# A planner that counts DMA landings later, keeps row loads and expert weights apart, and starts with the first q and k

## The chip, the cores and the metric

The kernel runs on one core of one Trainium2 chip. The metric is the device time of the program in microseconds (us). Three runs of the kernel before gave 535.44, 537.68 and 540.07 us; the median, 537.68, is what the change is measured against.

## The reference

Two stages, one behind the other. The first is attention over 8 batches, 8 heads, 576 positions and 64 channels, masked by blocks of 64; the second is a noisy top-2 router over 8 experts with two layers each.

```python
scores = q @ k.T / sqrt(64), masked where block(i) < block(j); attn = softmax(scores)
x = (attn @ v) as 4608 rows of 512
noisy = x @ w_gate + log1p(exp(x @ w_noise)) * noise
top2 = the two largest of noisy per row, with softmax weights over the two
out[row] = sum over its two experts e of weight * (relu(x[row] @ w1[e]) @ w2[e])
```

w1[e] is 512x1024, w2[e] is 1024x512, all inputs and the output are float32; the kernel computes its products in bfloat16.

## The kernel before

**Attention** goes through the batches 0 to 7. For each batch, six loads of q and k (`load_qk`, chunks c = 0, 1, 2) go out on GpSimd's queue (POOL) with a cast to bfloat16 into eight "raw" buffers; TensorE (PE) turns them (`turn`), VectorE (DVE) or ScalarE (ACT) copies the turned chunk to SBUF as Tq and Tk (`turn_copy`). V comes in five pieces on SyncE's queue (SP) as float32 into three "vst" buffers (`load_v`), and DVE or POOL casts each piece (`cast_v`). PE makes scores in twelve units and one small rest unit per batch, ACT takes their exponentials (`exps`), DVE zeroes the masked blocks (`mask`, L424), PE multiplies with V (`av_mm`, L439 and L449), DVE divides (`av_out`).

**Router.** After each pair of batches DVE computes the top two and every row's place in the list of its expert; POOL scatters each row twice into a table in DRAM (`scatter`, L586), xd[0] for batches 0 to 3 (half 0) and xd[1] for batches 4 to 7 (half 1). Behind each row lies a record of 16 bytes. The ends of the lists are cleared beforehand by eight DMAs from SP for each half (`clear_x`).

**Experts.** Each of 16 steps handles one expert for one half, in the order (0,0), (0,1), (0,2), (1,0), (1,1), (1,2), then (0,e), (1,e) for e = 3 to 7. A step loads 640 rows transposed from xd (`load_x`, L612, SP, two "xg" buffers), runs eight layer-1 groups of eight matmuls (`layer1`, L659) with a relu each (L668), and five layer-2 tiles (`layer2`, L675). The first product of a token is scaled (`y_early`, L683, ACT or DVE, three "y" buffers) and stored to DRAM by SP (`y_store`, L690); the second gathers the first by POOL (`gather`, L699), adds it on DVE (`y_late`, L710) and is scattered to the output by POOL (`y_out`, L717). The records of a half are read once (`load_rec`, L617, SP) and turned into row numbers and weights by DVE (`read_rec_a`, L625 to L634, and `read_rec_b`). Expert weights come in four loads each on POOL's queue with a cast to bfloat16 (`load_w`, L333); experts 0 to 2 have buffers of their own during attention, later ones reuse the space of attention.

**The order of the work** is not written by hand. `Plan` is a list scheduler that runs while the program is built: each operation has an engine (or a choice of two), a cost, operations that it comes after, buffers that it takes and gives, and a key (lower goes first). A DMA holds its engine for its cost, then its transfer takes `xfer` on one of two "wires" (POOL's or the rest), starting 1.2 after the issue, and counts as landed 1.0 after the wire is done. `behind` waits for another operation's start, `calm` holds an operation back while its wire is booked further ahead than that number. The planned times give only the order of each engine's instructions. On the chip an instruction waits for data and for buffers, never for a planned time; each engine takes its instructions strictly in that order, so one that waits holds up all behind it.

Of the kernel before, what the change touches and what calls it, by code (L numbers as in the profile page):

```python
# [19 lines left out]
class Plan:  # L20
# [4 lines left out]


    HOP = 0.08
    ISSUED = 1.2
    LANDED = 1.0
    WIDE = 1.15  # L30

# [3 lines left out]

    def add(self, eng, cost, fn=None, after=(), key=0.0, take=(), give=(), xfer=None, behind=(), calm=None):
        eng = () if eng is None else (eng,) if isinstance(eng, str) else tuple(eng)
        self.ops.append(dict(eng=eng, cost=cost, fn=fn, key=key, take=tuple(take), give=tuple(give),
                             xfer=xfer and xfer / self.WIDE, calm=calm, left=0, outs=[], next=[], start=None, by=None))
        n = len(self.ops) - 1  # L40
        for field, named in (("outs", after), ("next", behind)):
            for a in set(x for x in named if x is not None):
                self.ops[a][field].append(n)
                self.ops[n]["left"] += 1
        return n

    def order(self):
        ops, free = self.ops, dict(self.pools)
        busy, ready, marks, ends = {}, {}, [], []
        wire = {True: 0.0, False: 0.0}  # L50

        def put(n):
# [6 lines left out]
        def may(o):  # L59
            if o["calm"] is not None and wire[o["eng"][0] == "POOL"] - t > o["calm"]:  # L60
                return False
            return all(free[p] > 0 for p in o["take"])

        def begin(n, t, e):
# [13 lines left out]
            if o["xfer"] is not None:  # L78
# [6 lines left out]
                end = wire[q] + self.LANDED  # L85
            heapq.heappush(ends, (end if e is None else end + self.HOP, n))

# [3 lines left out]
        t = 0.0  # L91
        while True:
# [37 lines left out]
            if ends:  # L130
                t = ends[0][0]
            elif any(ready.values()) and t < max(wire.values()):
                t = max(wire.values())
            else:
                break
# [7 lines left out]
def kernel(  # L143
# [100 lines left out]
    zeros = [zrow[32 * i:32 * i + 32, 0:4 * DR] for i in range(4)]  # L244

    def setup_first():
        make_identity(nc, ident)
# [348 lines left out]

    def clear_x(half):
        flat = xd[half].rearrange("(e r) c -> e r c", e=E)[:, ZR:CAP, :].rearrange("e (p a) c -> e p (a c)", a=4)
        for e in range(E):
            nc.sync.dma_start(out=flat[e], in_=zeros[e % 4])  # L600

# [161 lines left out]

    UB = 3 * HP + 1

    def unit(b, n):
# [3 lines left out]

    add("POOL", 0.6, setup_first, key=-100)
    o_pool = add("POOL", 2.0, setup_pool, key=-30)
    o_vec = add("DVE", 2.5, setup_vector, key=-1)
# [11 lines left out]
    xr_new = {}  # L785
    prev_router = None
    av_all, noi = {}, {}
    qk_free = {}
    last_units = []
# [4 lines left out]
    for b in range(B):  # L794
# [7 lines left out]
        for c in range(3):  # L802
            for x in "qk":
                ld = add("POOL", 0.76 if c < 2 else 0.6, lambda b=b, x=x, c=c: load_qk(b, x, c),
                         key=u0 - 20 + c, take=["raw"], xfer=1.6 if c < 2 else 0.4,
                         after=[units[b - 2, (2, 0)]] if b > 1 else [])
                turned[x, c] = ld
        need = {0: u0, 1: u0 + 3, 2: u0 + 6}
        got = {}
        for c in range(2):  # L810
            for x in "qk":
                pe = add("PE", 0.55, lambda b=b, x=x, c=c: turn(b, x, c), after=[turned[x, c], o_new],
                         key=need[c] - 5, take=["tr"], give=["raw"])
                n = got[x, c] = add(("DVE", "ACT"), (1.04, 1.0), None, after=[pe], key=need[c] - 5, give=["tr"])
                pl.ops[n]["fn"] = lambda b=b, x=x, c=c, n=n: turn_copy(b, x, c, pl.ops[n]["by"])
        pe = add("PE", 0.6, lambda b=b: turn_rest(b), after=[turned["q", 2], turned["k", 2], o_new],
                 key=need[2] - 5, take=["tr"], give=["raw", "raw"])
# [4 lines left out]
        for idx in range(5):  # L822
            ld = add("SP", 0.15, lambda b=b, idx=idx: load_v(b, idx), key=u0 - 20 + idx, take=["vst"],
                     xfer=1.2 if idx < 4 else 0.6, after=[units[b - 2, (0, 0)]] if b > 1 else [])
            n = cast[idx] = add(("POOL", "DVE"), (0.62, 0.5) if idx < 4 else (0.7, 0.6), None,
                                after=[ld, o_vb], key=u0 - 2, give=["vst"])
            pl.ops[n]["fn"] = lambda b=b, idx=idx, n=n: cast_v(b, idx, pl.ops[n]["by"])
        o_nz = add("SP", 0.2, lambda b=b: load_nz(b), key=u0, xfer=0.6,
                   after=[units[b - 1, (1, 0)]] if b else [o_cast])
# [3 lines left out]
        for n, un in enumerate(UNITS):  # L833
            key = u0 + n
            if un == "r":
                s = add("PE", 0.4, lambda b=b: scores_rest(b), key=key, take=["sc"], after=list(got.values()))
                units[b, "r"] = add("ACT", 0.44, lambda b=b: exps_rest(b), key=key, after=[s, o_e4], give=["sc"])
                continue
# [7 lines left out]
            if m >= 3:  # L846
                deps += [got["r"]]
            s = add("PE", 0.4, lambda b=b, m=m, p=p: scores(b, m, p), key=key, take=["sc"], after=deps)
            units[b, (m, p)] = add("ACT", 1.05, lambda b=b, m=m, p=p: exps(b, m, p), key=key,
# [28 lines left out]
        add(None, 0, key=u0, after=[pes[0, 4], pes[1, 4]], give=["esc4"])  # L878
        add(None, 0, key=u0, after=[units[b, (3, 2)]], give=["qk"])

        kr = u0 + UB + 1
# [22 lines left out]
        if b % 2:  # L904
# [7 lines left out]
            add(None, 0, key=kr, after=[rw, sh], give=["rt"])  # L912
            ss = [add("POOL", 1.0, lambda pb=pb, t=t, i=i: scatter(pb, t, i), after=[rw, sh], key=kr + (20 if b < 7 else 0),
                      xfer=0.36)
# [3 lines left out]
        if b % BH == BH - 1:  # L918
            tot = add("PE", 0.2, lambda half=half: totals(half), after=[sh], key=kr + 1, take=["av"])
            done_b[half] = add("DVE", 0.2, lambda half=half: totals_copy(half), after=[tot], key=kr + 1, give=["av"])  # L920
    for half in range(NH):
        add("SP", 0.8, lambda half=half: clear_x(half), key=2, after=[units[half, (2, 0)], o_vec], xfer=2.8)

# [25 lines left out]
    o_top = add(None, 0, open_top, key=0, after=end_av)  # L949
    rec_ops = {}  # L950
    for half in range(NH):
        lr = add("SP", 0.2, lambda half=half: load_rec(half), key=unit(6, 6) + 0.5, after=scat_ops[half], xfer=3.0)
        ra = add("DVE", 1.6, lambda half=half: read_rec_a(half), key=unit(6, 0), after=[lr, done_b[half], o_cast])
        rec_ops[half] = add("DVE", 1.8, lambda half=half: read_rec_b(half), key=unit(6, 0), after=[ra])
    st_ops = {i: [] for i in range(NH)}
    l2_of, wmarks = {}, {}
    last_g = last_2 = last_x = last_h = None
    for sn, (half, e) in enumerate(SEQ):
        kb = 1000 + 20 * sn
        lx = add("SP", 0.2, lambda half=half, e=e: load_x(half, e), key=unit(6, 6) + sn, take=["xg"],  # L960
                 after=scat_ops[half], behind=[last_x], xfer=3.7)
        last_x = lx
        o_h = add(None, 0, key=kb, take=["hs"], after=[lx, last_h])
        last_h = o_h
# [211 lines left out]
```

## Time and profile before

| | |
|---|---|
| median of 3 runs | 537.68 us |
| the profiled execution | 536.13 us, span 534.4 us |
| busy over the span | PE 419.3, POOL 287.0, ACT 256.2, PE weight loads 260.5, DVE 180.5 us |
| mean granted TensorE clock | 0.886 |
| DMA | 96.22 MB landed, mean 180 GB/s; 104384 of 143642 packets under 512 B |

The profile is of one execution. Its page cuts the span into 40 slices of 13.4 us, each digit the busy share of an engine in tenths. The other views used are: the timeline (start, length, engine, line, operation, tile, and in brackets how long the engine stood idle before it and what released it); the list of waits (engine, line, what it waited for, us in total, times, longest); and windows (busy time of each engine in a stretch, then the granted clock of TensorE as a share of full speed, the mean busy share of the 16 DMA engines, which passes 1 when packets of two queues overlap, and GB/s). PE is TensorE's matmuls, PEld its weight loads, SPq and POOLq the queues' own DMA issues.

### The profile page before, as it was taken

How to read it: one execution, taken by the hardware profiler on the slowest of the kernel's cores; microseconds unless marked ns; L12 is line 12 of the kernel's file. 1: busy time of each engine (PE TensorE's matmuls, PEld its weight loads, DVE VectorE, ACT ScalarE, POOL GpSimd, SP SyncE). 2: the span in 40 equal slices, each digit the busy share in tenths (PEclk: the TensorE clock that was granted, in tenths of full speed). 3: DMA queues.
4: the chain of work that ended last, by engine and by line, in shares of the span. 5: the costliest groups of instructions: out<-in, count | busy, mean ns of one | idle time of the engine just before them, and what ended most of it. 6: DMA issues, size and time to landing. Idle time of an engine off the chain costs nothing.

```text
span 534.4 us, 10377 instructions
## 1 busy us (share of the span) xinstructions
PE 419.3 (78%) x4092; PEld 260.5 (49%) x4111; DVE 180.5 (34%) x486; ACT 256.2 (48%) x344; POOL 287.0 (54%) x327
## 2 busy tenths in 40 slices
PE   2588777887760199979997979489959979999990
PEld 1366555655530077635654626255435545565550
DVE  3477588578560264013211121002113212112220
ACT  2478777488651066534534525155233534555220
POOL 7134357678724742776633656347544554557560
PEclk9779889589755589999999989879979989999996
DMA  9999997896999999859999697977949986677440
GB/s 163 185 204 164 192 208 170 192 196 174 231 98 135 157 149 159 247 127 203 200 236 210 132 214 110 203 151 211 206 145 209 206 229 203 209 226 233 148 136 32
DMA packets 143642, 96.22 MB, mean 180 GB/s; under 512 B 104384, under 2 KB 121792, under 8 KB 143584
## 3 DMA queue, kind: packets, MB, share of 16 engines
q0 software_dynamic: 38496, 54.74, 50.6%
q1 hardware_dynamic: 105088, 40.73, 37.5%
q8 instruction: 34, 0.56, 0.5%
q14 instruction: 24, 0.20, 0.1%
HBM read 80.56 MB, written 48.41 MB: 241 GB/s over the span
## 4 chain that ended last, share of the span: by engine, by line
PE 45%; DMA 25%; issue 9%; POOL 6%; DVE 5%; ACT 4%; SPq 3%; POOLq 0%; ACTq 0%; DVEq 0%
PE hp L659 19%; PE yp L675 17%; DMA yd<-ysb 7%; DMA rc<-xd 6%; DMA vst<-in_v_dram 5%; POOL xd L586 3%; DMA raw<-in_k_dram 3%; ACT esc L403 2%; PE av L439 2%; DMA raw<-in_q_dram 2%; DMA gbuf<-yd,grow 2%; PE sc L394 2%; POOL out_dram L717 2%; PE av L449 1%; SPq L612 1%
## 5 line engine op out<-in xcount | busy, mean ns | idle before, releaser
L659 PE MATMUL hp<-xg,w 128*128 128x320 bf16 x1024 | 150.8, 308 | 21.2 <-ACT hsb L668 21.2
L675 PE MATMUL yp<-w,hsb 128*128 128x512 bf16 x621 | 144.4, 385 | 10.6 <-DVE yo L710 9.6
L710 DVE SCALAR_TENSOR_TENSOR yo<-yp,wrow,gbuf 128x512 f32<-128x512 f32 x70 | 52.3, 750 | 252.8 <-ACT ysb L683 119.2
L659 PEld LDWEIGHTS <-w 128*128 128x128 bf16 x1024 | 102.3, 100 | 67.7 <-issue 22.2
L668 ACT ACTIVATE hsb<-hp 128x640 bf16<-128x640 f32 x128 | 89.6, 704 | 64.8 <-PE hp L659 64.4
L717 POOL DMA_INDIRECT out_dram<-yo,trow x70 | 70.8, 1011 | 92.2 <-DVE yo L710 73.7
L403 ACT ACTIVATE esc<-sc 128x1024 bf16<-128x1024 f32 x96 | 93.5, 1026 | 28.8 <-PE sc L394 28.5
L675 PEld LDWEIGHTS <-hsb 128*128 128x128 bf16 x640 | 63.1, 99 | 85.8 <-issue 17.7
L683 ACT ACTIVATE ysb<-yp,wrow 128x512 f32<-128x512 f32 x69 | 47.4, 687 | 111.4 <-PE yp L675 72.9
L586 POOL DMA_INDIRECT xd<-xr,slots x72 | 72.1, 1001 | 46.0 <-DVE ms L571 22.1
L699 POOL DMA_INDIRECT gbuf<-yd,grow x70 | 72.9, 1042 | 38.1 <-issue 21.4
L439 PE MATMUL av<-vt,esc 128*128 128x65 bf16 x640 | 31.4, 207 | 28.6 <-DVE esc L424 23.7
L394 PE MATMUL sc<-Tq,Tk 64*128 64x512 bf16 (+4 forms) x320 | 41.1, 343 | 15.2 <-ACT esc L403 7.4
L439 PEld LDWEIGHTS <-esc 128*128 128x128 bf16 x640 | 25.9, 106 | 36.6 <-DVE esc L424 24.8
L344 PE MATMUL tr<-ident,raw 128*64 128x128 bf16 x512 | 26.8, 265 | 19.0 <-DMA raw<-in_q_dram 15.7
L459 DVE TENSOR_TENSOR xr<-av,rden 128x256 bf16<-128x256 f32 (+1 forms) x80 | 33.9, 424 | 4.0 <-DMA xd<-xr,slots 1.2
L333 POOL DMA_DIRECT2D w<-in_moe_w_dram x32 | 25.2, 795 | 15.0 <-DMA w<-in_moe_w_dram 10.0
L344 PEld LDWEIGHTS <-raw 128*64 128x64 bf16 x512 | 20.7, 137 | 25.7 <-DMA raw<-in_q_dram 16.3
L312 POOL CAST vt<-vst 128x512 bf16<-128x512 f32 x14 | 8.5, 616 | 41.2 <-DMA vst<-in_v_dram 15.7
L394 PEld LDWEIGHTS <-Tk 64*128 64x128 bf16 x320 | 13.1, 100 | 27.2 <-issue 13.8
L458 DVE RECIPROCAL rden<-av 128x4 f32<-128x4 f32 (+1 forms) x80 | 14.1, 177 | 14.3 <-PE av L439 9.6
L449 PE MATMUL av<-vt,esc 128*64 128x65 bf16 x320 | 15.4, 211 | 4.0 <-DVE noisy L507 3.6
(120 smaller groups left out, 230.0 us busy)
## 6 DMA issues: line engine op xcount, KB each, us to landing
yd<-ysb SPq DMA_DIRECT2D x70, 256.0 KB, 2.9
w<-in_moe_w_dram POOLq DMA_DIRECT2D x32, 512.0 KB
vst<-in_v_dram SPq DMA_DIRECT2D x32, 256.0 KB, 7.9
raw<-in_q_dram POOLq DMA_DIRECT2D x16, 256.0 KB
raw<-in_k_dram POOLq DMA_DIRECT2D x16, 256.0 KB
xd<-gbuf SPq DMA_DIRECT2D x16, 130.0 KB, 7.2
xd<-xr,slots POOLq DMA_INDIRECT x72
gbuf<-yd,grow POOLq DMA_INDIRECT x70
```

Source lines behind the costliest of these rows:

```text
L344: nc.tensor.transpose(tp[64 * f:64 * f + 64, r * P:(r + 1) * P], raw[:, f, r * D:(r + 1) * D], ident)
L394: nc.tensor.matmul(out=sc[:, f, off:off + z - a], lhsT=kT[sl, m * S + jt * P:m * S + (jt + 1) * P], rhs=qT[sl, m * S + a:m * S + z], start ...
L403: nc.scalar.activation(out=escs[b, st][:, mm, :, piece * 512:(piece + 1) * 512], in_=scs.pop((b, m, piece)), func=AF.Exp, scale=scale)
L439: nc.tensor.matmul(out=av[:, f, mm, :], lhsT=esc[:, mm, f, c:c + P], rhs=vb[:, jt, h, :], start=(jt == 0), stop=(jt == idx))
L586: ins = nc.gpsimd.indirect_dma_start(out=xd[half].bitcast(I32), out_offset=bass.IndirectOffsetOnAxis(ap=slots[:, pb * TG + t, i:i + 1], ax ...
L659: nc.tensor.matmul(out=hp[:, n, 0:NW], lhsT=wload[e, 1][:, db, fb * P:(fb + 1) * P], rhs=xgs[half, e][:, db, n * NW:(n + 1) * NW], start=( ...
L668: nc.scalar.activation(out=o, in_=i, func=AF.Relu)
L675: nc.tensor.matmul(out=yp, lhsT=hs[half, e][:, fb, c * P:(c + 1) * P], rhs=wload[e, 2][:, fb, :], start=(fb == 0), stop=(fb == FB - 1))
L683: nc.scalar.activation(out=t, in_=yps[half, e, c], func=AF.Copy, scale=w)
L699: ins = nc.gpsimd.indirect_dma_start(out=g, out_offset=None, in_=yd[half][0:e * CAP], in_offset=bass.IndirectOffsetOnAxis(ap=grow[half][:, ...
L710: nc.vector.scalar_tensor_tensor(out=t, in0=yps[half, e, c], scalar=wrow[half][:, e, c:c + 1], in1=gslot.pop((half, e, c)), op0=ALU.mult, ...
L717: ins = nc.gpsimd.indirect_dma_start(out=out, out_offset=bass.IndirectOffsetOnAxis(ap=trow[half][:, e, c:c + 1], axis=0), in_=yos.pop((hal ...
```

## The change

The planner gets two more numbers for an operation. `late` is added to the planned landing of a DMA: 2.0 for q, k, V, noise and weight loads, 1.5 for stores and gathers of the first products, 3.0 for row loads, 5.0 for the record load. `kind` marks row loads of the first four steps ("x") and weight loads ("w"): in the plan none of one kind starts before the last of the other has landed, and a weight load also stands back while a row load could start. Weights of experts 1 and 2 are planned behind the row loads of the second and third step; the condition `calm` of expert 0's goes from 2 to 4. Row loads and record loads now cost SP 4.0 in the plan instead of 0.2. POOL starts with the two first loads (q and k, c = 0), then the identity matrix, the other four loads of batch 0, and then the constants; V of batch 0 is planned after the first turns, and q and k of batch 1 behind V of batch 0. The clears become single operations at batch 1 (half 0) and batch 4 (half 1) with `calm`, scatters wait for them and are planned 4.0 after their row numbers, and scores of a batch stand behind the rest unit of the batch before. What is computed, the DMAs and their sizes are the same.

```diff
-    WIDE = 1.15
+    WIDE = 1.1
...
         def may(o):
             if o["calm"] is not None and wire[o["eng"][0] == "POOL"] - t > o["calm"]:
+                return False
+            if o["kind"] and last["w" if o["kind"] == "x" else "x"] > t:
+                return False
+            if o["kind"] == "w" and any(ops[n]["kind"] == "x" and ops[n]["start"] is None and
+                                        all(free[p] > 0 for p in ops[n]["take"]) for _, n in ready.get("SP", ())):
                 return False
...
                 end = wire[q] + self.LANDED
-            heapq.heappush(ends, (end if e is None else end + self.HOP, n))
+                if o["kind"]:
+                    last[o["kind"]] = max(last[o["kind"]], end)
+            heapq.heappush(ends, (end + o["late"] + (0.0 if e is None else self.HOP), n))
...
-    add("POOL", 0.6, setup_first, key=-100)
-    o_pool = add("POOL", 2.0, setup_pool, key=-30)
+    o_ident = add("POOL", 1.2, setup_ident, key=-50)
+    o_first = add("DVE", 2.2, setup_first, key=-50)
+    o_pool = add("POOL", 2.0, setup_pool, key=-17)
...
                 ld = add("POOL", 0.76 if c < 2 else 0.6, lambda b=b, x=x, c=c: load_qk(b, x, c),
-                         key=u0 - 20 + c, take=["raw"], xfer=1.6 if c < 2 else 0.4,
-                         after=[units[b - 2, (2, 0)]] if b > 1 else [])
+                         key=u0 - 20 + c if b or c else -100, take=["raw"], xfer=1.6 if c < 2 else 0.4, late=LATE,
+                         after=[units[b - 2, (2, 0)]] if b > 1 else [], behind=[v_last] if b == 1 else [])
...
-            ld = add("SP", 0.15, lambda b=b, idx=idx: load_v(b, idx), key=u0 - 20 + idx, take=["vst"],
-                     xfer=1.2 if idx < 4 else 0.6, after=[units[b - 2, (0, 0)]] if b > 1 else [])
+            ld = v_last = add("SP", 0.45, lambda b=b, idx=idx: load_v(b, idx), key=u0 - 20 + idx, take=["vst"],
+                              xfer=1.2, late=LATE, after=[units[b - 2, (0, 0)]] if b > 1 else [] if b else [turn0],
+                              behind=[v_last])
...
+        if b % BH == 1 - half:
+            cleared = [add("SP", 0.3, lambda half=half, e=e: clear_x(half, e), key=u0 + 5 + e,
+                           after=[units[b, (2, 0)], o_vec], xfer=0.36, calm=2.0) for e in range(E)]
...
-            ss = [add("POOL", 1.0, lambda pb=pb, t=t, i=i: scatter(pb, t, i), after=[rw, sh], key=kr + (20 if b < 7 else 0),
+            routed = add(None, 4.0, after=[rw, sh])
+            ss = [add("POOL", 1.05, lambda pb=pb, t=t, i=i: scatter(pb, t, i), after=[routed, *cleared], key=kr + (20 if b < 7 else 0),
...
-    for half in range(NH):
-        add("SP", 0.8, lambda half=half: clear_x(half), key=2, after=[units[half, (2, 0)], o_vec], xfer=2.8)
...
-                       behind=[prev, marks[n]], calm=calm, xfer=(2.7, 3.1)[n // 2])
+                       behind=[prev, marks[n]], calm=calm, xfer=3.3, late=2.0, kind="w")
-    for e in range(NWE):
-        weights(e, lambda: wE, [units[2 + e, (m, 0)] for m in range(4)], unit(6, 0) + e)
...
-        lr = add("SP", 0.2, lambda half=half: load_rec(half), key=unit(6, 6) + 0.5, after=scat_ops[half], xfer=3.0)
+        lr = add("SP", 4.0, lambda half=half: load_rec(half), key=unit(6, 6) + 0.5, after=scat_ops[half], xfer=3.0, late=5.0)
...
+    weights(0, lambda: wE, [units[2, (m, 0)] for m in range(4)], unit(6, 0), calm=4)
...
-        lx = add("SP", 0.2, lambda half=half, e=e: load_x(half, e), key=unit(6, 6) + sn, take=["xg"],
-                 after=scat_ops[half], behind=[last_x], xfer=3.7)
+        lx = add("SP", 4.0, lambda half=half, e=e: load_x(half, e), key=unit(6, 6) + sn, take=["xg"],
+                 after=scat_ops[half], behind=[last_x], xfer=3.7, late=3.0, kind="x" if sn < 4 else None)
         last_x = lx
+        if sn in (1, 2):
+            weights(sn, lambda: wE, [lx] * 4, unit(6, 0) + sn)
...
-                            after=st_ops[half] + [rec_ops[half]], behind=[last_g], xfer=0.7)
+                            after=st_ops[half] + [rec_ops[half]], behind=[last_g], xfer=0.7, late=1.5)
...
-                new.append(add("SP", 0.15, lambda half=half, e=e, c=c: y_store(half, e, c), after=[ye],
-                               key=kb, give=["y"], xfer=0.7))
+                new.append(add("SP", 0.35, lambda half=half, e=e, c=c: y_store(half, e, c), after=[ye],
+                               key=kb, give=["y"], xfer=0.7, late=1.5))
```

## Rows read from the trace of the kernel before

**Rows 1.** The page's 40 slices: PE's busy share and the DMA engines', in tenths

```profile
PE   2588777887760199979997979489959979999990
DMA  9999997896999999859999697977949986677440
```

**Rows 2.** The timeline around the long stop of PE, SP's queue first, then POOL, DVE, PE

```profile
146.27 6.21 SPq L612 DMA_TRANSPOSE xg<-xd  x1
152.53 5.79 SPq L617 DMA_DIRECT2D rc<-xd  x1
...
148.29 1.43 POOL L333 DMA_DIRECT2D w<-in_moe_w_dram  x2
...
179.95 0.82 POOL L333 DMA_DIRECT2D w<-in_moe_w_dram  x1
...
183.25 0.22 DVE L625 TENSOR_SCALAR rf<-rc 128x120 f32<-128x120 int32 x1 [24.06 <-DMA rc<-xd]
...
184.88 0.84 PE L439 MATMUL av<-vt,esc 128*128 128x65 bf16 x12 [23.44 <-DVE esc L424]
```

**Rows 3.** Windows of 4 us: busy us of each engine, then clock, DMA share, GB/s

```profile
152.00:156.00 4.00, 1.89 (x26) 1.46 (x26) 3.18 (x14) 0.00 (x0) 0.00 (x0) 0.50 1.34 79
156.00:160.00 4.00, 2.88 (x25) 1.29 (x25) 2.60 (x15) 3.99 (x6) 0.89 (x1) 0.50 1.43 58
184.00:188.00 4.00, 3.12 (x43) 2.13 (x44) 3.42 (x16) 0.38 (x1) 3.39 (x4) 0.50 1.18 213
216.00:220.00 4.00, 4.00 (x21) 1.84 (x20) 0.00 (x0) 1.38 (x2) 3.08 (x4) 1.00 1.05 344
228.00:232.00 4.00, 4.00 (x23) 2.08 (x22) 0.00 (x0) 1.71 (x3) 2.95 (x3) 1.00 0.47 166
```

**Rows 4.** The timeline of the second record load and its reader

```profile
236.04 0.38 SPq L617 DMA_DIRECT2D rc<-xd  x1
...
243.26 0.42 DVE L625 TENSOR_SCALAR rf<-rc 128x120 f32<-128x120 int32 x1
```

**Rows 5.** The line of the row loads: time from issue to landing over all 16

```profile
DMA to landing us min/median/max: 4.8/10.7/25.7
```

**Rows 6.** The page's DMA issues: the weight loads

```profile
w<-in_moe_w_dram POOLq DMA_DIRECT2D x32, 512.0 KB
```

**Rows 7.** The timeline of PE where the second step's first layer begins

```profile
209.00 1.25 PE L659 MATMUL hp<-xg,w 128*128 128x320 bf16 x8
```

**Rows 8.** The timeline of the start: SP, POOL, DVE, and PE's turns and scores

```profile
0.92 2.02 SPq L301 DMA_DIRECT2D vst<-in_v_dram  x3
...
3.33 0.91 POOL L291 DMA_DIRECT2D raw<-in_q_dram  x1
...
5.97 1.12 DVE L312 CAST vt<-vst 128x512 bf16<-128x512 f32 x3
...
8.83 1.06 PE L344 MATMUL tr<-ident,raw 128*64 128x128 bf16 x16 [8.83 <-DMA raw<-in_q_dram]
...
14.82 1.06 PE L344 MATMUL tr<-ident,raw 128*64 128x128 bf16 x16
22.27 1.04 PE L394 MATMUL sc<-Tq,Tk 64*128 64x512 bf16 x6 [6.39 <-DVE Tq L355]
```

**Rows 9.** The list of PE's waits: PE behind the relu's output

```profile
PE hp L659 <- ACT hsb L668: 21.2, 5, 8.7
```

**Rows 10.** The timeline of one such stop: SP's row load, ACT, PE

```profile
328.16 8.78 SPq L612 DMA_TRANSPOSE xg<-xd  x1
...
346.31 0.69 ACT L683 ACTIVATE ysb<-yp,wrow 128x512 f32<-128x512 f32 x1 [11.10 <-DMA yd<-ysb]
...
348.77 1.49 PE L659 MATMUL hp<-xg,w 128*128 128x320 bf16 x5 [8.66 <-ACT hsb L668]
```

**Rows 11.** The list of all waits: VectorE's casts behind V

```profile
DVE vt L312 <- DMA vst<-in_v_dram: 13.8, 4, 10.2
DVE vt L316 <- DMA vst<-in_v_dram: 13.1, 8, 2.6
```

More of the change, by code (lines that the diff above doesn't have):

```diff
@@ L34, in __init__, with add @@
         self.pools = dict(pools)
-    def add(self, eng, cost, fn=None, after=(), key=0.0, take=(), give=(), xfer=None, behind=(), calm=None):
+    def add(self, eng, cost, fn=None, after=(), key=0.0, take=(), give=(), xfer=None, behind=(), calm=None, late=0.0, kind=None):
         eng = () if eng is None else (eng,) if isinstance(eng, str) else tuple(eng)
         self.ops.append(dict(eng=eng, cost=cost, fn=fn, key=key, take=tuple(take), give=tuple(give),
-                             xfer=xfer and xfer / self.WIDE, calm=calm, left=0, outs=[], next=[], start=None, by=None))
+                             xfer=xfer and xfer / self.WIDE, calm=calm, late=late, kind=kind, left=0, outs=[], next=[], start=None, by=None))
         n = len(self.ops) - 1
@@ L50, in order @@
         wire = {True: 0.0, False: 0.0}
+        last = {"x": 0.0, "w": 0.0}
         def put(n):
@@ L131, in order @@
                 t = ends[0][0]
-            elif any(ready.values()) and t < max(wire.values()):
-                t = max(wire.values())
+            elif any(ready.values()) and t < max(*wire.values(), *last.values()):
+                t = max(*wire.values(), *last.values())
             else:
@@ L244, with setup_ident @@
     zeros = [zrow[32 * i:32 * i + 32, 0:4 * DR] for i in range(4)]
+    def setup_ident():
+        make_identity(nc, ident)
     def setup_first():
-        make_identity(nc, ident)
         for i in range(2):
@@ L595, in scatter, with clear_x @@
         scat[half].append(ins.ins.name)
-    def clear_x(half):
+    def clear_x(half, e):
         flat = xd[half].rearrange("(e r) c -> e r c", e=E)[:, ZR:CAP, :].rearrange("e (p a) c -> e p (a c)", a=4)
-        for e in range(E):
-            nc.sync.dma_start(out=flat[e], in_=zeros[e % 4])
+        nc.sync.dma_start(out=flat[e], in_=zeros[e % 4])
     xgs, hs, hps, yps, ysb, yos, grow, trow, wrow = ({} for _ in range(9))
@@ L764 @@
     UB = 3 * HP + 1
+    LATE = 2.0
     def unit(b, n):
@@ L785 @@
     xr_new = {}
-    prev_router = None
+    prev_router = v_last = None
     av_all, noi = {}, {}
-    qk_free = {}
+    rest = {}
     last_units = []
@@ L811 @@
             for x in "qk":
-                pe = add("PE", 0.55, lambda b=b, x=x, c=c: turn(b, x, c), after=[turned[x, c], o_new],
+                pe = add("PE", 0.55, lambda b=b, x=x, c=c: turn(b, x, c), after=[turned[x, c], o_new, o_ident],
                          key=need[c] - 5, take=["tr"], give=["raw"])
+                if c == 0:
+                    turn0 = pe
                 n = got[x, c] = add(("DVE", "ACT"), (1.04, 1.0), None, after=[pe], key=need[c] - 5, give=["tr"])
                 pl.ops[n]["fn"] = lambda b=b, x=x, c=c, n=n: turn_copy(b, x, c, pl.ops[n]["by"])
-        pe = add("PE", 0.6, lambda b=b: turn_rest(b), after=[turned["q", 2], turned["k", 2], o_new],
+        pe = add("PE", 0.6, lambda b=b: turn_rest(b), after=[turned["q", 2], turned["k", 2], o_new, o_ident],
                  key=need[2] - 5, take=["tr"], give=["raw", "raw"])
@@ L822 @@
         for idx in range(5):
-            ld = add("SP", 0.15, lambda b=b, idx=idx: load_v(b, idx), key=u0 - 20 + idx, take=["vst"],
-                     xfer=1.2 if idx < 4 else 0.6, after=[units[b - 2, (0, 0)]] if b > 1 else [])
+            ld = v_last = add("SP", 0.45, lambda b=b, idx=idx: load_v(b, idx), key=u0 - 20 + idx, take=["vst"],
+                              xfer=1.2, late=LATE, after=[units[b - 2, (0, 0)]] if b > 1 else [] if b else [turn0],
+                              behind=[v_last])
             n = cast[idx] = add(("POOL", "DVE"), (0.62, 0.5) if idx < 4 else (0.7, 0.6), None,
-                                after=[ld, o_vb], key=u0 - 2, give=["vst"])
+                                after=[ld, o_vb, o_first], key=u0 - 2, give=["vst"])
             pl.ops[n]["fn"] = lambda b=b, idx=idx, n=n: cast_v(b, idx, pl.ops[n]["by"])
-        o_nz = add("SP", 0.2, lambda b=b: load_nz(b), key=u0, xfer=0.6,
+        o_nz = add("SP", 1.0, lambda b=b: load_nz(b), key=u0, xfer=0.4, late=LATE,
                    after=[units[b - 1, (1, 0)]] if b else [o_cast])
@@ L835 @@
             if un == "r":
-                s = add("PE", 0.4, lambda b=b: scores_rest(b), key=key, take=["sc"], after=list(got.values()))
+                s = rest[b] = add("PE", 0.4, lambda b=b: scores_rest(b), key=key, take=["sc"], after=list(got.values()))
                 units[b, "r"] = add("ACT", 0.44, lambda b=b: exps_rest(b), key=key, after=[s, o_e4], give=["sc"])
@@ L847 @@
                 deps += [got["r"]]
-            s = add("PE", 0.4, lambda b=b, m=m, p=p: scores(b, m, p), key=key, take=["sc"], after=deps)
+            s = add("PE", 0.4, lambda b=b, m=m, p=p: scores(b, m, p), key=key, take=["sc"], after=deps,
+                    behind=[rest.get(b - 1)])
             units[b, (m, p)] = add("ACT", 1.05, lambda b=b, m=m, p=p: exps(b, m, p), key=key,
```

## The prediction

> **What bounds the kernel now.** I read the page's slices first, to find where PE, with 419 us the busiest engine, is not busy. Three places stand out [rows 1]: the first two slices, slice 13 (160 to 174 us, digit 0), and single digits of 4, 5 and 7 in the second half. The DMA digits show something else: nearly 9 throughout until the last quarter, so transfers are a resource to be shared, and a gain in one place may be taken back in another.
>
> The timeline around slice 13 names the stop [rows 2]. PE stands for 23.44 us behind the mask at L424. The mask needs nothing new; it is queued on DVE behind the first instruction of the record reader (L625), which waits 24.06 us for the record load. SP issued the first row load at 146.27 and the record load at 152.53; DVE was at L625 at 183.25 - 24.06 = 159.2, and the records were there at 183.25, 37.0 us after the first row load began. Why so late: POOL issued two weight loads of expert 1 at 148.29, into the middle of the row load. The windows show what the mixture does [rows 3]: from 152 to 160 the engines are fully booked (share 1.34 and 1.43) and land only 79 and 58 GB/s, against 344 GB/s at 216. The comparison is the second record load, with no weight load beside its first microseconds: issued at 236.04, its reader ran at 243.26 without a wait, so it took at most 7.2 us [rows 4].
>
> **The change, part by part.** The sum is against the profiled execution, 536.13 us, which stands 1.55 below the median.
>
> *The record wait.* Two edits act on it. The plan's own numbers (order only, no times of the chip): before, the records count as landed 0.2 + 1.2 + 3.7/1.15 + 3.0/1.15 + 1.0 = 8.2 after the first row load starts; now the row load holds SP for 4.0, the record load ends at 8.0, its wire at 8.0 + 1.2 + 3.0/1.1 = 11.9, landing with 1.0 and `late` 5.0 at 17.9. So L625 moves some 9.7 back in DVE's order, behind mask and divisions that no longer stand behind it. And weights of expert 1 can't be planned before the second row load has landed: 8.0 + 4.0 + 1.2 + 3.7/1.1 + 1.0 = 17.6 after the first began, instead of 2 us after it. Apart, a row load took 4.8 us at best and 10.7 in the median [rows 5], the record load 7.2 at most: records at 12 to 18 us after the first row load. DVE used to arrive at 12.9 and now arrives near 22.6. The wait goes: **-23.4**, lower gains under the rivals.
>
> *The clock behind it.* PE's granted clock was 0.50 (1.2 GHz) through the stop and still in 184 to 188, with 3.12 us of matmuls [rows 3]; at full clock these take half. **-1.5** (0 to -3).
>
> *Weights late.* What is late next is expert 1. Before, its four loads went out from 148.29 to 179.95 [rows 2], and PE began the second step at 209.00 [rows 7], 62.7 after the first row load. Without the stop PE arrives at 62.7 - 23.4 = 39.3. Loads that start at 17.6 at the old spacing, (179.95 - 148.29)/3 = 10.6 each, would end near 17.6 + 31.7 + 3 = 52: 13 us late. Four loads land 4 x 512 KB [rows 6]; at the 166 GB/s of an ordinary stretch [rows 3] that is 12.6: ready near 31, early. The range is 0 to +13; I take **+4**, nearer the unmixed end, because the mixing is what the edit ends.
>
> *The start.* POOL now issues q and k before its constants; q went out at 3.33 and PE turned it at 8.83, 5.5 later [rows 8]. From about 0.9 that gives 6.4: -2.4. SP has no data to wait for, so V's first loads still go out at 0.92 beside q; "ahead of V" holds in the plan alone. The identity's two POOL instructions, behind two issues, are hidden by the wait for q. Six q and k issues now precede the constants; DVE's cast of these comes later, while DVE has nothing else. Then PE stood 6.39 us because DVE held V's casts ahead of the copy to Tq; its turn was over at 15.88 and scores came at 22.27. With V counted 2.0 later, copies come first: up to -6.4. Against it: V's three buffers were emptied from 5.97 on; casts placed behind the copies come some 8 us later, and so do the next V loads. Range -9 to +8; I take **-3**, as the engines are booked from the first slice [rows 1].
>
> *First products in the expert stage.* PE waited 21.2 us in five stops for a relu [rows 9]. In one of them a row load held SP's queue for 8.78 us from 328.16, the stores came behind it, ACT stood 11.10 us for a free store buffer with the next step's relus behind it, and PE stood 8.66 [rows 10]. The plan saw none of that: a row load cost 0.2, a store landed 0.15 + 1.2 + 0.7/1.15 + 1.0 = 3.0 after its turn. Now the row load costs 4.0 and the store lands 1.5 later, so the fourth product is planned behind two or so relus of the next step, each of which feeds 1.09 us of PE work (the plan's cost of a group). Five stops by 2.2 is 11; all 21.2 at most; a worse order could cost 5. I take **-6**, half of the 11, because moved products delay others.
>
> *V's ring.* Casts stand later everywhere. DVE waits 26.9 us in all for V [rows 11]; most of the lateness is time that was waited before. **+2** (0 to +36, see below).
>
> *At nothing:* the clears (same sixteen DMAs, at other batches; V's landings cover them; 0 to +3 if V stands behind them), expert 0's `calm` of 4 (the same four loads, earlier, beside q and k; 0 to +4), `routed` and the wait of scatters for the clears (done long before), scores behind the rest unit (same order). The end of the kernel is untouched.
>
> Sum: -23.4 - 1.5 + 4 - 3 - 6 + 2 = -27.9; 536.13 - 27.9 + 1.55 = **510**.
>
> **The rivals.** *Apart on paper only (R1).* Nothing on the chip makes POOL wait for the row loads. If POOL reaches expert 1's weights while they are in flight, records come 37.0 after the start again, DVE arrives at 22.6, and 14.4 us of waiting remain: -9.0, with the other terms -1 + 0 - 3 - 6 + 2: 537.7 - 17 = **521**. Against it: POOL has the scatters of the third pair ahead, which wait for the router; for it: planned and real times differ everywhere.
>
> *The same bytes (R2).* The record wait is traded one for one for PE waiting on expert weights, and the relus' stops stay: all else but the clock returned, 537.7 - 1.5 = **536**. For it: booked engines [rows 1]. Against it: 58 GB/s in the mixture against 344 apart, and a share of 0.47 at 228 [rows 3], room that later work can use. The Trainium skill (DMA: Bandwidth & Descriptors, "Issuing engines are not separate DMA queues") speaks for R2: DMAs from different issuing engines run on the same 16 DMA engines and interleave, so that keeping two queues apart wins no bandwidth. By that rule the sum would be R2's; the trace agrees that they share, and not that sharing is free.
>
> *V starves attention (R3), slower.* 40 V loads pass three buffers, 13.3 turns of the ring. If V's landing is what limits attention, each turn costs the planned 2.0 + 0.3 (issue 0.45 instead of 0.15) more, the first 8: 8 + 12.3 x 2.3 = 36, and 537.7 - 23.4 - 1.5 - 0 + 36 = **549**. It decides from 1.9 us a turn on (24.9/13.3). For it: DVE's 13.8 and 13.1 us behind V [rows 11]; against it: later casts mean that DVE copies q and k in that time instead.
>
> **How the numbers follow.** Forecast 0.62, R1 0.16, R2 0.10, R3 0.12. The forecast's own range is 494 to 526: the relus' whole 21.2 and the whole start gain on one side, 13 us of late weights and a start without gain on the other. The range to hold 8 in 10 reaches to R2: 494 to 536; outside are R3 and some of the forecast's lower edge. A measurement can tell about 1%, 5.4 us: faster (forecast and R1) 0.78, within it (R2) 0.10, slower (R3) 0.12.
>
> **What would show it.** In the changed profile: DVE's wait at L625 under 5 us, slices 12 and 13 of PE at 6 or more, no window near 58 GB/s around the first row load (R1: weight loads within 10 us of it, 10 us or more at L625). First turn of PE before 7.5. PE behind relus under 15 us in all. PE waiting on weights by more than 13 us would be R2; attention's last matmul not 15 us earlier than before, with DVE, POOL or PE waits on V grown, would be R3. The forecast is wrong if the record wait is gone and the time is not.

## The result, and the profile after

Four runs of the changed kernel took 511.34 to 523.88 us, median 515.76; beside them the kernel before, with a fourth run, took 538.09 (535.44 to 540.07). The ratio is 0.956 [0.947, 0.965]: faster, by 22.3 us where 27.9 were forecast, and 5.8 above the predicted 510. The profiled execution is the longest of the four, 523.88 (span 522.2), 8 us over the median. Ratios, here and below, are of undisturbed runs alone; where none is given, too few were left, and the median of all runs stands with their range.

The page's slices of PE answer to [rows 1], counted from 1 as there: slice 13 went from 0 to 8, slice 2 from 5 to 7, and the second half still has single digits of 4 to 7.

```profile
PE   2788894869868997996699996999898497599890
```

Cutting both executions at the last score of attention (194.8 before, 168.5 after) splits the result. Windows; columns as in [rows 3]. First the kernel before:

```profile
0.00:194.80 194.80, 125.25 (x2298) 89.56 (x2298) 114.02 (x349) 115.35 (x140) 107.97 (x147) 0.78 1.03 176
194.80:534.40 339.60, 294.06 (x1798) 170.95 (x1813) 66.44 (x137) 140.87 (x205) 179.05 (x180) 0.95 0.80 183
```

The changed kernel:

```profile
0.00:168.50 168.50, 127.55 (x2298) 90.71 (x2298) 109.56 (x346) 117.29 (x143) 95.47 (x136) 0.83 0.97 185
168.50:522.20 353.70, 298.84 (x1797) 171.87 (x1813) 84.27 (x162) 123.59 (x180) 189.15 (x193) 0.92 0.89 184
```

The last score comes 26.3 us earlier, and the rest, the expert stage, takes 14.1 longer: PE is busy 4.8 us more at a clock of 0.92 instead of 0.95, and idle 54.9 instead of 45.5. So 26.3 were gained and a good half of it was given back in this execution.

**At the old stop.** SP's queue, POOL's weight loads and the record reader, which answer to [rows 2]:

```profile
149.07 0.37 SPq L628 DMA_DIRECT2D rc<-xd  x1
149.50 38.03 SPq L623 DMA_TRANSPOSE xg<-xd  x3
...
143.94 0.82 POOL L345 DMA_DIRECT2D w<-in_moe_w_dram  x1
...
165.19 0.79 POOL L345 DMA_DIRECT2D w<-in_moe_w_dram  x1
...
164.98 0.27 DVE L636 TENSOR_SCALAR rf<-rc 128x120 f32<-128x120 int32 x1
...
170.64 0.38 DVE L436 MEMSET esc<- 64x384 uint32 x1
```

The reader runs without a wait, at most 15.9 us after the record load's issue. Two things differ from before beside the weights: SP issues the record load *ahead* of the first row load, and only one pair of masks stands behind the reader (170.64), where three pairs stood before, behind L625 at 183.25 (the first of each pair):

```profile
184.45 0.38 DVE L424 MEMSET esc<- 64x384 uint32 x1
...
187.71 0.38 DVE L424 MEMSET esc<- 64x384 uint32 x1
...
197.07 0.38 DVE L424 MEMSET esc<- 64x384 uint32 x1
```

**PE's waits** (engine, tile, line, released by: us in total, times, longest):

```profile
PE hp L670 <- DVE hsb L681: 16.8, 4, 9.9
...
PE yp L686 <- DMA w<-in_moe_w_dram: 7.3, 2, 5.3
...
PE hp L670 <- DMA w<-in_moe_w_dram: 3.3, 1, 3.3
...
PE av L451 <- DVE esc L436: 1.3, 2, 0.8
PE hp L670 <- ACT hsb L679: 1.2, 2, 1.0
```

The mask wait fell from 23.44 [rows 2] to 1.3. The relu wait of [rows 9] has not gone; it moved from ACT (21.2 before, 1.2 now) to DVE (16.8), and waits on weights are new (10.6). The longest relu stop, on DVE, POOL and PE:

```profile
396.02 1.00 POOL L728 DMA_INDIRECT out_dram<-yo,trow  x1 [0.31 <-issue]
...
409.99 1.41 DVE L721 SCALAR_TENSOR_TENSOR yo<-yp,wrow,gbuf 128x512 f32<-128x512 f32 x2 [16.15 <-DMA out_dram<-yo,trow]
411.32 0.81 DVE L681 TENSOR_SCALAR hsb<-hp 128x640 bf16<-128x640 f32 x1
...
412.19 3.92 PE L670 MATMUL hp<-xg,w 128*128 128x320 bf16 x16 [9.88 <-DVE hsb L681]
```

DVE waits 16.15 us for a free output buffer, the relu is next in its order, and PE stands 9.88 behind it. DVE's waits for output buffers grew threefold; first the kernel before, then the changed one:

```profile
DVE yo L710 <- DMA out_dram<-yo,trow: 20.3, 7, 10.4
```

```profile
DVE yo L721 <- DMA out_dram<-yo,trow: 60.6, 17, 16.1
```

Why the buffer came free so late here was not tested. Ahead of the stop stands the same mixture as at the old one [rows 2], which the change keeps apart only for the first four steps: a row load and, 0.6 us later, a weight load. The windows beside them show a full share and little landed, as in [rows 3]:

```profile
386.06 12.28 SPq L623 DMA_TRANSPOSE xg<-xd  x1
...
386.64 0.81 POOL L345 DMA_DIRECT2D w<-in_moe_w_dram  x1
```

```profile
390.00:394.00 4.00, 4.00 (x20) 1.82 (x19) 1.90 (x3) 1.37 (x2) 2.71 (x3) 1.00 1.28 61
394.00:398.00 4.00, 4.00 (x27) 2.41 (x26) 0.00 (x0) 0.70 (x1) 3.08 (x4) 1.00 1.22 65
```

Before, all 128 relus ran on ACT; the changed plan gives 14 to DVE (line L681 in the groups by line: busy range of one in ns, from when to when):

```profile
L681 DVE TENSOR_SCALAR hsb<-hp x14: 814/816/826, 236.1 to 473.5; 128x640 bf16<-128x640 f32 x14
```

### The profile page after: what moved, and what is told of

It reads as the page before. It is cut to its first block, busy times and chain, and to the rows that moved or that the text cites. A ratio compares the mean times of both kernels' runs of the same rounds, so it can differ in the third digit from the quotient of the medians.

```text
span 522.2 us, 10391 instructions
## 1 busy us (share of the span) xinstructions
PE 426.4 (82%) x4091; PEld 262.6 (50%) x4111; DVE 193.8 (37%) x507; ACT 240.9 (46%) x322; POOL 284.6 (55%) x328
## 4 chain that ended last, share of the span: by engine, by line
issue 29%; DMA 22%; POOL 21%; PE 18%; DVE 4%; ACT 2%; POOLq 1%; SPq 0%; DVEq 0%; ACTq 0%
DMA vst<-in_v_dram 7%; PE hp L670 7%; POOL gbuf L710 6%; DMA gbuf<-yd,grow 6%; POOL xd L598 6%; POOL out_dram L728 5%; PE yp L686 5%; DMA yd<-ysb 4%; DMA w<-in_moe_w_dram 2%; PE av L451 2%; DMA raw<-in_q_dram 1%; POOL w L345 1%; PE sc L406 1%; ACT esc L415 1%; PE av L461 1%
## 5 line engine op out<-in xcount | busy, mean ns | idle before, releaser
L670 PE MATMUL hp<-xg,w 128*128 128x320 bf16 x1024 | 150.9, 306 | 21.3 <-DVE hsb L681 16.8
L686 PE MATMUL yp<-w,hsb 128*128 128x512 bf16 x620 | 149.7, 394 | 20.3 <-DVE yo L721 10.8
L679 ACT ACTIVATE hsb<-hp 128x640 bf16<-128x640 f32 x114 | 79.9, 703 | 96.3 <-PE hp L670 95.9
L686 PEld LDWEIGHTS <-hsb 128*128 128x128 bf16 x640 | 64.2, 100 | 99.0 <-issue 33.9
L415 ACT ACTIVATE esc<-sc 128x1024 bf16<-128x1024 f32 x96 | 92.7, 1026 | 30.0 <-PE sc L406 15.5
L694 ACT ACTIVATE ysb<-yp,wrow 128x512 f32<-128x512 f32 x60 | 41.0, 687 | 97.8 <-PE yp L686 62.2
L406 PE MATMUL sc<-Tq,Tk 64*128 64x512 bf16 (+4 forms) x320 | 42.8, 347 | 11.9 <-ACT esc L415 11.5
L451 PE MATMUL av<-vt,esc 128*128 128x65 bf16 x640 | 34.3, 212 | 8.2 <-DVE xr L471 5.7
L451 PEld LDWEIGHTS <-esc 128*128 128x128 bf16 x640 | 28.1, 109 | 18.2 <-DVE xr L471 7.5
L356 PEld LDWEIGHTS <-raw 128*64 128x64 bf16 x512 | 20.3, 135 | 21.3 <-DMA raw<-in_q_dram 14.1
L303 POOL DMA_DIRECT2D raw<-in_q_dram x16 | 11.9, 744 | 12.3 <-PE tr L356 10.5
L681 DVE TENSOR_SCALAR hsb<-hp 128x640 bf16<-128x640 f32 x14 | 11.3, 819 | 16.9 <-PE hp L670 16.8
```

The costliest lines, as they stand in the source:

```text
L356: nc.tensor.transpose(tp[64 * f:64 * f + 64, r * P:(r + 1) * P], raw[:, f, r * D:(r + 1) * D], ident)
L406: nc.tensor.matmul(out=sc[:, f, off:off + z - a], lhsT=kT[sl, m * S + jt * P:m * S + (jt + 1) * P], rhs=qT[sl, m * S + a:m * S + z], start ...
L415: nc.scalar.activation(out=escs[b, st][:, mm, :, piece * 512:(piece + 1) * 512], in_=scs.pop((b, m, piece)), func=AF.Exp, scale=scale)
L451: nc.tensor.matmul(out=av[:, f, mm, :], lhsT=esc[:, mm, f, c:c + P], rhs=vb[:, jt, h, :], start=(jt == 0), stop=(jt == idx))
L670: nc.tensor.matmul(out=hp[:, n, 0:NW], lhsT=wload[e, 1][:, db, fb * P:(fb + 1) * P], rhs=xgs[half, e][:, db, n * NW:(n + 1) * NW], start=( ...
L679: nc.scalar.activation(out=o, in_=i, func=AF.Relu)
```

## Experiments

Three groups of runs, each kernel timed beside the kernel before on the same chip. In the first two groups the whole kernel ran some 12% longer (median before: 609.2 and 604.9 us) than in the third (539.9) and in the first comparison (538.1); so times are compared within a group.

### First group: the parts alone

**The changed kernel again**, no edit.

> The changed kernel once more, for a profile beside the experiments of this chip. All theories: 512 to 518 us, no wait over 5 us at the record reader, attention's last score matmul some 26 us earlier than before the change.

580.1 us (577.6 to 586.8), ratio 0.962 [0.952, 0.972]. The gain holds where everything takes longer; the expected 512 to 518 us do not.

**The separation alone**, in the kernel before (the edit in words):

```diff
+    kind="w" on weight loads, kind="x" on row loads of steps 0 to 3, and their two rules in may()
-    weights of experts 0 to 2 planned during attention
+    weights of expert 0 there, of experts 1 and 2 behind the second and third row load
```

> The kernel before with one thing of the change: row loads of the first four steps and weight loads never in flight together in the plan, experts 1 and 2 planned behind row loads. In the programs' order the record load then also stands ahead of the first row load on SP. Theory A (mixing with weights makes the records late): the 23 us stop of PE is gone, 515 to 520 us. Theory B (VectorE's place for the record reader decides; here it stands even earlier in VectorE's order than before): a stop of 10 us or more stays, 527 us or more.

589.4 us (576.4 to 594.0, 4 runs; before 609.2). The reader does not wait for records; as in the changed kernel, the record load also went ahead of the first row load, so this edit does not move one thing alone.

**The record load's lateness alone:**

```diff
-lr = add("SP", 0.2, ... xfer=3.0)
+lr = add("SP", 4.0, ... xfer=3.0, late=5.0)
```

> The kernel before with one thing of the change: the record load costs 4.0 in the plan and lands 5.0 later, so VectorE's record reader stands 14 instructions later; order on SP and POOL around it as before. Theory A (mixing): records land some 37 us after the first row load as before, a stop of 10 to 15 us stays, 526 to 531 us. Theory B (place on VectorE): the stop is gone, 513 to 518 us.

611.7 us (596.8 to 616.1, 4 runs): no gain. The reader moved behind two more pairs of masks and still waited 12.8 us; the stop changed its victim, since the divisions for the router stand behind the reader now. The reader's row, and PE's wait:

```profile
206.65 0.22 DVE L633 TENSOR_SCALAR rf<-rc 128x120 f32<-128x120 int32 x1 [12.79 <-DMA rc<-xd]
```

```profile
PE lg L497 <- DVE xr L467: 12.8, 1, 12.8
```

**Only the order on SP**, record load ahead of the first row load, weights mixed in as before:

```diff
-key=unit(6, 6) + 0.5, after=scat_ops[half], xfer=3.0)
+key=unit(6, 6) - 0.5, after=scat_ops[half], xfer=3.0)
```

> The kernel before with the record load one place earlier on SP, ahead of the first row load; weight loads of expert 1 stay where they are, beside it. Theory A (mixing with weights slows whatever SP has in flight): records still come 15 us or more after the issue, a stop of 5 to 12 us stays, 522 to 532 us. Theory C (the record load is late because the row load lies ahead of it in SP's queue): the stop is gone, 513 to 518 us, with weights mixed in as before.

604.2 us (595.7 to 608.5), ratio 0.995 [0.986, 1.004]. The record load went out at 172.21 and its reader waited only 5.73 us, although weight loads were issued from 1.6 later on. PE shows no wait behind the mask over 0.2, and 46.8 us behind the relus: the stop can be gone and the time not.

```profile
172.21 0.37 SPq L617 DMA_DIRECT2D rc<-xd  x1
...
187.82 0.22 DVE L625 TENSOR_SCALAR rf<-rc 128x120 f32<-128x120 int32 x1 [5.73 <-DMA rc<-xd]
...
173.81 2.19 POOL L333 DMA_DIRECT2D w<-in_moe_w_dram  x3
```

### Second group: one part of the change undone

**The changed kernel**, once more beside them.

> The changed kernel beside the next three: 0.955 to 0.965 of the time before, on whatever chip this is.

571.9 us (563.8 to 575.7), ratio 0.950 [0.939, 0.960].

**Without the separation:** `kind` ignored, weights planned as before.

```diff
-late=late, kind=kind, left=0
+late=late, kind=None, left=0
```

> The changed kernel without the separation: weights of experts 0 to 2 planned as before the change, kinds ignored; records and all landings still counted late. Theory A (separation does it): most of the gain is lost, 0.980 to 1.000 of before, and the record reader waits 8 us or more again or attention's last scores come 15 us later than in the changed kernel. Theory B' (later places on the engines do it together): 0.955 to 0.968.

564.2 us (550.0 to 569.3): not slower than the change beside it. The theory that most of the gain hangs on the separation fell. The row load is again ahead of the record load, and the reader, with one pair of masks behind it as in the change, did not wait; but here it came to its place 37.1 us after the record load's issue (166.29 to 203.36), so this run does not try it.

**With the start as before:**

```diff
-o_ident = add("POOL", 1.2, ..., key=-50); first q and k at -100; V after [turn0], behind [v_last]
+o_ident = add("POOL", 0.6, ..., key=-100); first q and k at u0 - 20 + c; V as before
```

> The changed kernel with the start as before: constants first on POOL, V and q and k of batch 1 not held behind. Theory S1 (the start's gain of 7 us in the first batch is kept to the end): 7 us slower than the changed kernel, 1.3% . Theory S2 (transfers bound attention and take it back by batch 4): within 3 us of the changed kernel.

588.5 us (580.9 to 589.1), ratio 0.985 [0.977, 0.993]: 16.7 us above the changed kernel. The start is no small term there; in the profiles 8.6 of it stand before the last score (206.1 with the change, 214.7 here).

**With the expert stage's landings as before:**

```diff
-row loads of steps 4 to 15: cost 4.0, late=3.0; gather late=1.5; y store 0.35, late=1.5
+row loads of steps 4 to 15: cost 0.2; gather; y store 0.15
```

> The changed kernel with the expert stage planned as before: stores and gathers without the extra landing, row loads from the fifth step on at 0.2 with nothing added, stores at 0.15. Theory E1 (counting them later saves PE's stops behind relus, as predicted): 6 us slower than the changed kernel or more. Theory E2 (the stops only move to other producers, among them VectorE): within 3 us, either way.

603.4 us (598.5 to 620.5), ratio 1.009 [1.000, 1.017]: the whole gain is gone, 31.5 us. The last score comes at 205.1, with the change at 206.1, so the loss is in the expert stage. ACT behind the stores, PE behind the relus:

```profile
PE hp L670 <- ACT hsb L679: 56.5, 20, 14.2
...
ACT ysb L694 <- DMA yd<-ysb: 45.6, 7, 17.6
```

The changed kernel beside it, the same two waits:

```profile
PE hp L670 <- ACT hsb L679: 18.5, 13, 4.5
...
ACT ysb L694 <- DMA yd<-ysb: 7.4, 2, 4.9
```

### Third group: what the stop and the stage do alone

**The kernel before**, no edit, for its profile.

> The kernel before, unchanged, profiled on the chip that the other runs of this call use, because the second experiment's losses appeared in the expert stage and not at the record load. Theory R (the record stop is what the change removes): DVE waits 15 us or more at L625 and PE behind the mask about as long, PE waits behind the relus (L659 on L668) 15 to 25 us. Theory E (the expert stage's late landings are what it removes): PE waits behind the relus 40 us or more and ACT waits 30 us or more for free store buffers, the record wait being the smaller part. Both theories: the same time as before, ratio 1.00.

539.8 us, one run. Its waits show both stops, the record's and the relus':

```profile
ACT ysb L683 <- DMA yd<-ysb: 54.3, 14, 13.3
PE hp L659 <- ACT hsb L668: 32.5, 6, 10.3
DVE rf L625 <- DMA rc<-xd: 20.9, 2, 20.6
PE av L439 <- DVE esc L424: 20.2, 2, 20.0
```

Neither expectation fits alone: the record stop is nearly as large as in the first profile (20.0 against 23.4), and ACT's wait for store buffers is over 30 as well.

**Only the expert stage's landings**, in the kernel before (the edit above, the other way round).

> The kernel before with only the expert stage's landings planned later: row loads of steps 4 to 15 cost SP 4.0 and land 3.0 later, stores cost 0.35 and land 1.5 later, gathers land 1.5 later; start, record load, weights, clears and scatters as before. Theory E: this alone gives most of the gain, ratio 0.94 to 0.96, PE behind the relus under 25 us, ACT behind the stores under 10 us. Theory R: the record stop stays (15 us or more at L625), ratio 0.98 to 1.00. A third way (the parts only help together, as the row load apart alone did little): ratio 0.97 to 0.99 with the relu waits down but the time taken up by PE's waits on weights or gathers.

529.0 us (509.3 to 545.5; before 539.9, 529.0 to 546.7): the ranges overlap, so the times alone do not show a gain. The record stop stays, and the waits in the stage shrink:

```profile
DVE rf L633 <- DMA rc<-xd: 26.2, 1, 26.2
PE av L447 <- DVE esc L432: 26.0, 2, 25.7
...
PE hp L667 <- ACT hsb L676: 13.4, 2, 12.0
...
ACT ysb L691 <- DMA yd<-ysb: 10.7, 6, 2.9
```

From the last score on it takes 333.7 us where the kernel before took 346.3: 12.6 less, and 5.9 less than the 339.6 of its first profile. This lies between the expectations: some gain is likely with the stop in place, and the stage is not all of it.

**Without separation and without the record's lateness:** both edits undone.

```diff
-late=late, kind=kind; lr: cost 4.0, late=5.0
+late=late, kind=None; lr: cost 0.2
```

> The changed kernel without the separation of row loads and weights and without the record load's lateness (L623 and L628 planned as before); start and expert stage as changed. If the record load's lateness is what took the place of the separation in the run without it (which was no slower than the change): the wait at L625 is back with 10 us or more, and the time is 10 us or more above the run without the separation alone, ratio 0.95 to 0.97. If neither matters beside the start and the expert stage: the same as the run without the separation, ratio 0.92 to 0.945, no wait of over 5 us at L625.

525.6 us (513.5 to 528.5), below all runs of the kernel before (529.0 to 546.7). The two parts meant for the stop are out, a weight load runs beside the row load, the records take 14.8 us from their issue and their reader waits 8.4 us, and yet PE waits behind the mask for 1.5 us in all:

```profile
144.93 10.13 SPq L623 DMA_TRANSPOSE xg<-xd  x1
155.12 2.78 SPq L628 DMA_DIRECT2D rc<-xd  x1
...
145.87 0.71 POOL L345 DMA_DIRECT2D w<-in_moe_w_dram  x1
...
169.90 0.22 DVE L636 TENSOR_SCALAR rf<-rc 128x120 f32<-128x120 int32 x1 [8.39 <-DMA rc<-xd]
175.50 0.38 DVE L436 MEMSET esc<- 64x384 uint32 x1 [1.29 <-ACT esc L415]
```

Again one pair of masks stands behind the reader. The wait at L636 came back as the first expectation had it, but only 8.4 of its 10, and it costs PE next to nothing here.

**Without the separation, again.**

> The changed kernel without the separation alone, once more and with more rounds, as the version that may beat both: its runs were at 564 us where the change had 572 and the kernel before 605. If the separation costs time by holding weights back: ratio 0.925 to 0.945, below the change's 0.950 to 0.962. If the difference was scatter: ratio 0.945 to 0.965.

520.2 us (506.1 to 525.9), 0.964 of the kernel before: the second expectation. The medians put it 5 below the kernel above it, with ranges that overlap almost wholly. In its profile (508.2 us) the reader waited, and PE behind the mask with it, 9.3 us in all where the change has 1.3:

```profile
176.07 0.22 DVE L636 TENSOR_SCALAR rf<-rc 128x120 f32<-128x120 int32 x1 [9.63 <-DMA rc<-xd]
...
178.02 0.84 PE L451 MATMUL av<-vt,esc 128*128 128x65 bf16 x12 [7.58 <-DVE esc L436]
```

So a third of the old stop can come back without the separation; the time does not show it. Against the change itself it is 7.6 lower in the second group and was not run beside it in the third: no slower, but not shown to be faster.

## Why the prediction was right, and where it was not

**The record wait** went, and the size was right: from the start to the last score the terms were -23.4 - 1.5 - 3 + 2 = -25.9, and 26.3 came. The signs named for it were there: no wait at the reader, slices 12 and 13 at 6 and 8, and around the first row load (148 to 164) windows of 4 us that land 107 GB/s or more. The reason given was half wrong. The step failed where the prediction took SP's order as unchanged (row load, then records) and the separation as the cure. In the plan the row load, which has a `kind`, stood back behind expert 0's fourth weight load (143.94), the record load has none, and so it went first; with `kind` alone the order is the same, and with `kind` ignored the row load is ahead again. Nor is the separation what takes away most of the stop: the two kernels of the third group without it have their last scores near 168 and 174 us (168.5 in the change), and one of them lacks the lateness too. What they share with the changed kernel is the reader's place: one pair of masks behind it instead of three. What the separation, with the order that it brings, takes away is the rest: without it the reader still waited 8.4 and 9.6 us in these two, and PE up to 7.6 behind it. The other half of the step, that the reader moves behind mask and divisions, is what the runs bear out. Which of the remaining edits (row loads at cost 4.0, the scatters' 4.0, the earlier start) moves the reader without the record's own lateness was not tried alone; the clears and the new order of scores were taken back in no run. And no run put the whole stop back into the changed kernel: its share of the gain is read from the trace, not from a time.

Nor is the place enough by itself: with the lateness alone the reader moved and a 12.8 us wait stopped the router's product.

**Apart on paper (R1)** did not happen: POOL came to expert 1's weights 15.7 us after the first row load.

**Weights late** were to cost +4 of 0 to +13, for expert 1. They cost nothing there: its four loads went out from 165.19 to 179.19, 4.7 us apart instead of 10.6, and PE began the second step at 183.24, 33.7 after the first row load, without a wait. The 10.6 us that PE did wait for weights come later, where the forecast had no term: first behind expert 2's, then at 450.04 (5.28) and 489.38 (1.97). The last weight load, issued at 482.34 (419.83 before), shows weights late to the end of the kernel.

```profile
208.05 10.17 PE L670 MATMUL hp<-xg,w 128*128 128x320 bf16 x52 [3.31 <-DMA w<-in_moe_w_dram]
```

**The start and V's ring** were mis-sized in opposite ways. PE's first turn came at 7.78 instead of 8.83 (before 7.5 was forecast), the stop of 6.39 [rows 8] is gone, and the router product of the first batch is 7.2 us earlier (42.78 to 35.63), that of the third 9.7 (82.50 to 72.84). By the fifth all is given back (123.92 to 124.27), in two stops, one behind q and one behind V:

```profile
87.47 1.06 PE L356 MATMUL tr<-ident,raw 128*64 128x128 bf16 x16 [5.32 <-DMA raw<-in_q_dram]
108.48 1.06 PE L451 MATMUL av<-vt,esc 128*128 128x65 bf16 x16 [5.00 <-DVE xr L471]
...
107.45 0.43 DVE L324 CAST vt<-vst 128x512 bf16<-128x512 f32 x1 [6.24 <-DMA vst<-in_v_dram]
```

So the two terms, -3 and +2, were -9.7 up to the third batch and some +10 behind it: together the forecast's -1 against +0.35. That they cancel is luck. Of the +10 only the stop behind V is like rival R3, in small; the one behind q was in no term. In the second group, where everything took longer, the start was worth 16.7 us.

**First products.** The mechanism is the one forecast: with the landings nominal, ACT stands behind the stores (45.6 us) and PE behind the relus (56.5), and the whole gain is lost. Its size was not: 31.5 us there, 12.6 or 5.9 in the stage when done alone, and in the first comparison, where -6 was forecast, the relu waits fell by 3.2, from 21.2 to 18.0, over the forecast's bound of 15. The prediction missed that relus may go to either engine: the changed plan gives 14 of them to DVE (8 with the late landings alone, 2 with the landings nominal, 4 without the separation), whose order holds additions that wait for an output buffer. The landing of those output scatters is the one of this stage's buffers that the change leaves nominal; counting it later too was not tried.

**The same bytes (R2).** The bytes did not set the end: the change gained 4.4%. The rule itself (the Trainium skill, DMA: Bandwidth & Descriptors, "Issuing engines are not separate DMA queues": transfers of different queues interleave on the same 16 engines, so that spreading them wins no bandwidth) is measured by no run here, and the times agree with it: undoing the separation cost none in the second group (564.2 against 571.9). What the separation buys is one landing: the reader's wait of 8.4 and 9.6 us.

**What stays open.** A good half of the gain was given back in the profiled execution: for the expert stage the terms were +4 - 6 = -2, and +14.1 came. This execution gained 12.3 us on the profiled one before, the medians 22.3, so the hit of the total is not borne out term by term. The ends of the forecast's own range do not follow from its terms either: the whole gain of relus and start gives 489, late weights and a start without gain 522. The 14.1 us in the expert stage are 9.3 of idle PE, the weights' 10.6 being the largest new wait, and 4.8 of PE at a clock of 0.92 instead of 0.95. How much of this the executions at 511 to 518 had is not known; only the longest was profiled. Whether the kernel before had the record stop in the two slower groups was not seen either, as it was profiled in neither.

## What to carry to other kernels

A stop behind a late transfer can be made small by moving the reader behind the work that others need, even if the transfer stays late (here 1.5 and 9.3 us of 23.7 were left); count first what is queued behind it, since the stop can move to the next in line. When a planner's landing times are corrected, correct all that free a buffer of the same stage, since the stop may move to one left nominal (DVE's wait for output buffers went from 20.3 to 60.6 us), and look at which engine gets the work that may go to either. Price an order of transfers by redoing the plan, with every operation that the new rule does not cover: here one without a `kind` went ahead of one that has it.

## What was not expected of the hardware

The same kernels took 11 to 13% longer in two groups of runs than in the others (changed kernel 571.9 and 580.1 against 515.8). The first and the third group ran on the same chip, so it is not the chip alone. The instructions themselves took as long: an exponential 1026 ns on ACT, a relu 703 ns in both. Up to the third batch the changed kernel ran nearly the same (its router product at 72.91 and 72.84); then come stretches in which PE and ACT hardly work and the DMA engines are not full. Two windows of the slower execution, columns as above:

```profile
140.00:150.00 10.00, 3.15 (x40) 2.09 (x40) 0.82 (x3) 2.78 (x5) 6.08 (x8) 0.50 0.45 101
190.00:200.00 10.00, 2.81 (x27) 1.49 (x27) 1.28 (x3) 1.80 (x2) 8.03 (x9) 0.50 0.84 169
```

The profile puts these to issue, or to another core or an unknown queue; what it was is not settled.

The issue of a transposing row load can hold its queue for long: in the changed kernel each took SP 2.5 to 12.3 us, in the kernel before up to 28.9 (from 158.37), while the record load ahead of the first took 0.37. What it waits for is not shown. The 38.03 us shown above for three row loads are no such time: the third was issued at 183.13, after SP had waited from 159.0 on for PE to be done with a buffer.
